# Attention and two gated MLPs on one core: a new instruction order from shaken latest-end times with named seeds

## The chip, the cores and the metric

The kernel runs on one core of one Trainium2 chip. The metric is the device time of one execution in microseconds, the median of three runs. An engine here is TensorE (PE, with its weight loads PEld), VectorE (DVE), ScalarE (ACT), GpSimd (POOL) or SyncE (SP, which issues the DMAs).

## The reference

Twelve heads of capped softmax attention for two batches of 448 tokens feed an RMS-normalised gated MLP and a second MLP, all in float32.

```python
scores = cap * np.tanh((scale * np.matmul(q, k.transpose(0, 1, 3, 2))) / cap)
attn = np.exp(scores - np.max(scores, axis=-1, keepdims=True))
attn = attn / (np.sum(attn, axis=-1, keepdims=True) + 1e-09)
x = tokens(np.matmul(attn, v))                      # 896 x 768
xn = x / np.sqrt(np.mean(x * x, axis=-1, keepdims=True) + 1e-06) * rms_g
g = xn @ w_gate                                     # 768 x 1536
h = (g * (1 / (1 + np.exp(-g))) * (xn @ w_val)) @ w_out
h2 = h @ w_in                                       # 768 x 2048
out = (h2 * (1 / (1 + np.exp(-h2)))) @ w_out2       # 2048 x 768
```

## The kernel before, in words

**Attention.** Twelve pairs of heads are worked on one after the other, overlapped. For a pair, PE computes scores in three chunks of 128 query rows for both heads (`qk`, L469: two products on half of the array's rows each) and one mixed chunk (L466); ACT takes the tanh (L476) and the exponential (L494); DVE caps and negates (`mx`, L484); PE transposes the probabilities (L559, L563, L561), DVE or ACT copies the transposes out (`ev`, L315), and PE multiplies them by the values (`pv`, L582: products on half of the array's columns, and L578). The row sums pass a small DVE operation (`guard`, L512) and a reciprocal; POOL spreads the reciprocals (L518, L523), and PE turns them (L529, L530). POOL also squares the results (L599, L600, L603), copies the mixed chunk's diagonal blocks (`diag`, L538) and computes the low parts of the first weights (L398).

**MLPs.** Products are made with float32r halves: each operand is split into a high part (a cast, L315) and a low part (a subtraction, L398, L675, L685), and one product is a triple of three matmuls (`passes`, L703; in the last matrix L1111). Seven products on sums of blocks take the place of eight (`group`); the sums of token blocks are called T1 to T4. Weights are loaded 768 columns at a time (`wraw`), unpacked by two ACT operations (L377, L380) and one DVE operation (L383), summed and split.

**What sets the order.** The kernel's operations are not emitted in the order of the code. The code records them in a `Plan` with costs for each engine that may run them, what they read and write, and which buffer they take. `place` lays them on the engines one by one: among those that can start within a small window it takes the one with the earliest due time (`prio`). `order` repeats this nine times, with due times that `dues` works back from the last placing, and keeps the placing whose last operation starts first. In the attention's plan 300 further tries add a random amount to 5% of the due times and keep what is no worse; the MLPs' plan (`rest`) has none. The instructions are then emitted in the order of the kept placing, and each engine runs its own in that order. A plan's costs set only the order and the choice of the engine; the chip keeps its own time. The first products of each MLP use `plain`, the others of this kind `group`; the gated MLP's output matrix, whose products go by `o` and a number, has its `mul` further down.

Of the kernel before, what the change touches and what calls it, by code (L numbers as in the profile page):

```python
# [2 lines left out]

# [25 lines left out]
CG = 12.0  # L29
WARM = 8  # L30
ROUNDS = 8
TRIES = 300
SHAKE = 2.0
SHARE = 0.05
XS = 0.5
PE = 6
TYH = 6.0
# [7 lines left out]
class Plan:  # L45
# [68 lines left out]
            due = min([end] + [ops[n]["prio"] for n in after[i]]) - cost  # L114
            o["prio"] = min(due, s) if e == "PE" else due

    def order(self, rounds=0, tries=0):

        users = self._link()
        best = None  # L120
        for n in range(rounds + 1):
            due = [o["prio"] for o in self.ops]
            out = self.place(users)
            if best is None or out[-1][0] < best[0][-1][0]:
                best = out, self.placed, due
            self.dues(users, self.placed)
        chance = random.Random(0)
        for n in range(tries):
            for o, due in zip(self.ops, best[2]):
                o["prio"] = due + (chance.gauss(0.0, SHAKE) if chance.random() < SHARE else 0.0)  # L130
            due = [o["prio"] for o in self.ops]
            try:
                out = self.place(users)
            except RuntimeError:
                continue
            if out[-1][0] <= best[0][-1][0]:
                best = out, self.placed, due
        self.placed = best[1]
        return best[0]

    def place(self, users):
# [84 lines left out]
def fused_kernel(ctx: ExitStack, tc: tile.TileContext, qkv, cap, g, wg, wv, wo, wi2, wo2, out):  # L226
# [61 lines left out]
    plan = Plan(TP, DUE, WIN, BIAS1)  # L288
# [458 lines left out]
        (sums if i else operands)(plan, u, v, 2 * i + 2)  # L747

    engines = {"PE": nc.tensor, "ACT": nc.scalar, "DVE": nc.vector, "Pool": nc.gpsimd, "SP": nc.sync, "none": None}
    order = plan.order(ROUNDS, TRIES)  # L750
    ends = max(n for n, (_, _, _, i) in enumerate(order) if plan.ops[i]["kind"] == "xe")
    for n, (_, _, e, i) in enumerate(order):
        plan.ops[i]["fn"](engines[e])
# [21 lines left out]
    def group(n, u, v, turn, x, outs, stag, pause=0):  # L775

        X, Y, Z, st = f"X_{n}", f"Y_{n}", f"Z_{n}", f"s_{n}"
        HK = KD // 2
        steps = (
            (X, f"w_{u}", 0, "11", True), (Z, f"w_{u}", DH, "21", True), (X, f"s_{u}", 0, "T2", False),  # L780
            (Y, f"w_{v}", 0, "T1", True), (X, f"s_{u}", DH, "T3", False), (X, f"w_{v}", DH, "T4", False),
            (Y, f"q_{u}", 0, "22", False),
        )
        c11, c12, c21, c22 = outs

        def product(n):
            ps, w, c, y, start = steps[n]
            for k in range(HK):
                def mul(e, k=k, n=n):
                    if start and k == 0:  # L790
                        bank(ps, ps[0])
                    passes(tl[ps][:, :S], w, c + k * P, (half(x(y, k), 0), half(x(y, k), 1)), start and k == 0, k == HK - 1, not start)

                op("mul", turn + 0.14 * n + 0.04 * k + (pause if n > 1 else 0), mul, {"PE": 0.595}, (f"h{w}", f"l{w}", x(y, k) + ".0", x(y, k) + ".1"), (ps,),
                   (take(ps, ps[0]),) if start and k == 0 else ())

        def keep(n, ps, i):
            def fn(e):
                if n == 0:
                    slot(st, stag)  # L800
                copy(e, f32(half(st, i)), tl[ps][:, :S])
            op("keep", turn + 0.1 * n, fn, {"ACT": 0.43, "DVE": 0.54}, (ps,), (f"{st}.{i}",), ((stag, 1, st),) if n == 0 else ())

        def add(ps, i, out):
            name, o, alloc = out
            op("add", turn, lambda e: nc.vector.tensor_add(o(), f32(half(st, i)), tl[ps][:, :S]), {"DVE": 0.54}, (ps, f"{st}.{i}"), (name,), alloc)

        product(0)
        keep(0, X, 0)
        product(1)  # L810
# [12 lines left out]
    def plain(n, u, v, turn, x, order, pauses=(0, 0, 0, 0)):  # L823

        HK = KD // 2
        left = {}
        at = 0
        for s, (c, tag, ys) in enumerate(order):
            ps = f"{tag}_{n}{c}"
            left[c] = left.get(c, 2)  # L830
            for y in ys:
                begin = left[c] == 2
                left[c] -= 1
                w, cols = f"w_{(u, v)[int(c[0]) - 1]}", DH * (int(y[0]) - 1)
                for k in range(HK):
                    def mul(e, k=k, y=y, ps=ps, w=w, cols=cols, begin=begin):
                        if begin and k == 0:
                            bank(ps, ps[0])
                        passes(tl[ps][:, :S], w, cols + k * P, (half(x(y, k), 0), half(x(y, k), 1)), begin and k == 0, k == HK - 1, not begin)

                    op("mul", turn + 0.14 * at + 0.04 * k + pauses[s], mul, {"PE": 0.595}, (f"h{w}", f"l{w}", x(y, k) + ".0", x(y, k) + ".1"), (ps,),
                       (take(ps, ps[0]),) if begin and k == 0 else ())
                at += 1
        return {c: f"{tag}_{n}{c}" for c, tag, _ in order}
# [93 lines left out]
    def both(n):  # L938
        return n + ".0", n + ".1"
# [42 lines left out]
    for i, n in enumerate(seq):  # L982
        tn = t0 + 0.857 * i
        pa, pb = PLACES[n]
        for x in {1: ("11",), 5: ("21", "22"), 2: ("12",)}.get(n, ()):
            for j in range(MH):
                convert(rest, ua(x, j), tn + 0.1 * j, to=atags[x].split()[j])
        for side, o, x, sign, y in SUMS.get(n, ()):
            if side == "a":
                for j in range(MH):  # L990
                    weight_sums(tn + 0.1 * j, f"wz_{ua(o, j)}", f"wz_{ua(x, j)}", sign, f"wz_{ua(y, j)}")
            else:
                for k in range(KH):
                    (ho, no), (hx, nx), (hy, ny) = (hb(z, k) for z in (o, x, y))
                    op("hsum", tn + 0.143 * k, lambda e, a=(ho, no), b=(hx, nx), c=(hy, ny): e.tensor_sub(*(f32(half(*z)) for z in (a, b, c))),
                       {"DVE": 0.54, "Pool": 1.1}, [f"{h}.{z}" for h, z in {(hx, nx), (hy, ny)} - {(ho, no)}], (f"{ho}.{no}",))
        for j in range(MH):
            weight_split(tn + 0.1 * j, ua(pa, j), f"o{n}_{j}", ("wh", "wl") if j < 2 else ("sh", "sl"))
        for k in range(KH):
            h, c = hb(pb, k)  # L1000
            halves(rest, ("hsh", "hsl"), tn + 0.143 * k, f"B{n}_{k}", btags[i % 2][k], (f"{h}.{c}", lambda h=h, c=c: f32(half(h, c))))
        bank_of = "XXZYXYXX"[n] if n != 2 else "Z"
        fresh = n in (1, 5, 2)
        for r in range(KH * MH):
            k, j = divmod(r, MH) if n != 4 else divmod(r, KH)[::-1]
            ps, w, x = f"{bank_of}_o{j}", f"o{n}_{j}", f"B{n}_{k}"

            def mul(e, k=k, ps=ps, w=w, x=x, fresh=fresh):
                if fresh and k == 0:
                    bank(ps, ps[0])  # L1010
                passes(tl[ps][:, :S], w, k * P, (half(x, 0), half(x, 1)), fresh and k == 0, k == KH - 1, not fresh)

            op("mul", tn + 0.0476 * r, mul, {"PE": 0.595}, (f"h{w}", f"l{w}", *both(x)), (ps,), (take(ps, ps[0]),) if fresh and k == 0 else ())
        for j in range(MH):
            X, Y, Z, tj = f"X_o{j}", f"Y_o{j}", f"Z_o{j}", tn + 0.7
            y0, y1 = f"y0_{j}", f"y1_{j}"
            if n == 1:
                evac("keep", tj, X, yf(0, j, 0), y0 + ".0", (ytags[0][j], y0))
            elif n == 6:
                evac("keep", tj, X, yf(0, j, 1), y0 + ".1")  # L1020
            elif n == 7:
                evac("keep", tj, X, yf(1, j, 0), y1 + ".0", (ytags[1][j], y1))
                evac("add", tj, Y, yf(1, j, 0), y1 + ".0", acc=True)
            elif n == 2:
                evac("add", tj, Z, yf(0, j, 0), y0 + ".0", acc=True)
            elif n == 3:
                evac("add", tj, Y, yf(0, j, 1), y0 + ".1", acc=True)
            else:
                evac("y", tj, X, yf(1, j, 1), y1 + ".1") if n == 4 else None
# [73 lines left out]
    def tokens_mul(turn, ps, a, w, k, start, stop, reads, more=False):  # L1103
# [6 lines left out]
            for r, (y, x) in enumerate(((ah, wh), (ah, wl), (al, wh))):  # L1110
                nc.tensor.matmul(out=tl[ps][:, :DH], lhsT=y, rhs=x, start=start and r == 0, stop=stop and r == 2, skip_group_check=more)  # L1111

        op("mul", turn, mul, {"PE": 0.52}, (f"h{w}", f"l{w}", *reads), (ps,), (take(ps, ps[0]),) if start else ())

    def rest_mul(turn, n, m, w, k, start, stop):
        g, _, _, c, i = rest_tile(m)
# [96 lines left out]
            evac("o", tn, f"Z_r{int(n == 3)}", o, name, (ktags[3], r) if n == 2 else (stile[0], r), w=DH)  # L1213
            store(tn, 2 * TH2, int(n == 3), o, name)

    for _, _, e, i in rest.order(ROUNDS):
        rest.ops[i]["fn"](engines[e])


# [59 lines left out]
```

## Time and profile before

| | |
|---|---|
| median of 3 runs | 596.53 us (596.52 to 596.63) |
| span of the profiled execution | 595.1 us |
| median less that span | 1.4 us |
| PE busy | 585.7 us (98%) |
| DVE busy | 512.1 us (86%) |
| ACT busy | 451.1 us (76%) |
| POOL busy | 58.7 us (10%), in the attention alone |

The span runs from the first to the last instruction of the one profiled execution; what lies around it belongs to the measured time as well. Busy times of PE are modelled at their ends, so a stretch can be counted busy and still hold a short wait; the distance from one matmul's start to the next tells more. The attention ends and the MLPs begin at about 143 us.

### The profile page before, as it was taken

To read this page: it belongs to the slowest core of one execution; us is meant where nothing else is said; L and a number is where in the kernel's file an instruction comes from. 1 tells how busy PE (TensorE), PEld (TensorE's weight loads), DVE (VectorE), ACT (ScalarE), POOL (GpSimd) and SP (SyncE) were. 2 spreads that over 40 slices of the span, in tenths; PEclk is the share of its full clock that TensorE was granted. 3 is DMA by queue.
4 is the path that set the end of the run, shared out by engine and by line. 5 is a ranking of instruction groups with operands and counts; after the bars stand their busy time and mean duration, and the time that the engine had idled before them with its cause. 6 is when DMAs were issued, how large, how long until landed. Compare 5 with 4: busy or idle time off the path is not lost.

```text
span 595.1 us, 8525 instructions
## 1 busy us (share of the span) xinstructions
PE 585.7 (98%) x3056; PEld 495.5 (83%) x3056; DVE 512.1 (86%) x934; ACT 451.1 (76%) x800; POOL 58.7 (10%) x92
## 2 busy tenths in 40 slices
PE   8999999999999999999999999999999999999997
PEld 4555565557889999999999998998999999999997
DVE  4799997994999989888699999999877898999991
ACT  5999878983858777776698685777888899986641
POOL 1234561552000000000000000000000000000000
PEclk9999999999999999999999999999999999999999
DMA  7123311310024435443445200423534455440101
GB/s 265 54 106 107 107 56 53 139 75 0 2 106 160 160 108 168 150 143 123 160 167 187 72 0 2 159 61 114 197 113 159 156 209 178 155 145 1 41 26 68
DMA packets 15626, 66.22 MB, mean 111 GB/s; under 512 B 1888, under 2 KB 3680, under 8 KB 15584
## 3 DMA queue, kind: packets, MB, share of 16 engines
q1 hardware_dynamic: 15552, 65.67, 31.3%
q8 instruction: 24, 0.39, 0.3%
q14 instruction: 18, 0.15, 0.1%
q0 software_dynamic: 32, 0.00, 0.0%
HBM read 62.92 MB, written 2.75 MB: 110 GB/s over the span
## 4 chain that ended last, share of the span: by engine, by line
PE 88%; DVE 7%; ACT 3%; issue 1%; DMA 1%; SPq 0%; DVEq 0%; ACTq 0%
PE X L703 28%; PE Y L703 16%; PE Z L703 9%; PE X L1111 8%; PE av L582 5%; PE pt L559 5%; PE Y L1111 5%; PE s L469 5%; PE Z L1111 2%; PE s L466 2%; PE av L578 1%; PE pt L563 1%; PE pt L529 1%; DVE wl L398 1%; DMA x<-in_qkv 1%
## 5 line engine op out<-in xcount | busy, mean ns | idle before, releaser
L380 ACT ACTIVATE wraw<-wraw 128x768 uint32<-128x768 uint16 x68 | 61.8, 908 | 0.0
L703 PE MATMUL X<-q,sh 128*128 128x448 f32 x198 | 56.5, 365 | 0.6 <-DVE q L685 0.6
L484 DVE TENSOR_SCALAR_CACHE_REDUCE p<-p,ncap 128x448 f32<-128x448 f32 x72 | 45.9, 673 | 6.5 <-ACT p L476 6.3
L398 DVE TENSOR_TENSOR wl<-wz,wh 128x768 fp32r<-128x768 f32 x47 | 44.8, 954 | 6.4 <-ACT wh L315 6.3
L703 PE MATMUL X<-p,wh 128*128 128x448 f32 x174 | 49.8, 367 | 0.0
L315 ACT CAST wh<-wz 128x768 fp32r<-128x768 f32 x46 | 38.3, 834 | 12.0 <-DVE wz L418 4.5
L703 PE MATMUL X<-q,wh 128*128 128x448 f32 x162 | 46.2, 366 | 0.6 <-ACT p L315 0.6
L383 DVE SCALAR_TENSOR_TENSOR wz<-wz,wraw 128x768 uint32<-128x768 uint32 x44 | 42.0, 955 | 4.0 <-ACT wraw L380 3.8
L315 DVE COPY pe<-pt 128x448 f32<-128x448 f32 x72 | 41.3, 619 | 4.1 <-PE pt L563 3.7
L315 ACT COPY p<-X 128x448 f32<-128x448 f32 x45 | 24.0, 532 | 26.9 <-PE X L703 25.9
L703 PE MATMUL Z<-p,wh 128*128 128x448 f32 x150 | 42.9, 367 | 0.0
L377 ACT ACTIVATE wz<-wraw 128x768 f32<-128x768 f32 x44 | 40.1, 911 | 3.8 <-DMA wraw<-in_wi 1.6
L315 ACT CAST q<-p 128x448 fp32r<-128x448 f32 (+1 forms) x54 | 29.0, 547 | 17.8 <-PE X L1111 5.9
L476 ACT ACTIVATE p<-s,tscl 128x896 f32<-128x896 f32 x36 | 34.9, 1004 | 9.7 <-PE s L469 9.6
L703 PEld LDWEIGHTS X<-q,sh 128*128 128x128 f32 x198 | 37.2, 188 | 4.2 <-DVE q L685 1.0
L315 ACT CAST p<-p 128x448 fp32r<-128x448 f32 (+1 forms) x50 | 27.1, 552 | 12.6 <-DVE p L693 4.7
L703 PE MATMUL X<-q,sl 128*128 128x448 f32 x99 | 36.2, 366 | 0.0
L703 PEld LDWEIGHTS X<-p,wh 128*128 128x128 f32 x174 | 32.5, 188 | 2.8
L469 PE MATMUL s<-x 64*128 64x448 f32 x144 | 34.0, 574 | 0.3 <-ACT p L476 0.3
L703 PEld LDWEIGHTS X<-q,wh 128*128 128x128 f32 x162 | 30.3, 188 | 3.6 <-ACT p L315 1.0
L703 PE MATMUL X<-p,wl 128*128 128x448 f32 x87 | 31.8, 366 | 0.0
L582 PE MATMUL av<-pe,x 128*64 128x448 f32 x144 | 31.4, 552 | 0.0
(257 smaller groups left out, 1654.3 us busy)
## 6 DMA issues: line engine op xcount, KB each, us to landing
wraw<-in_wo SPq DMA_DIRECT2D x28, 768.0 KB, 4.3
wraw<-in_wi SPq DMA_DIRECT2D x16, 768.0 KB, 4.3
wraw<-in_wg SPq DMA_DIRECT2D x12, 768.0 KB, 5.8
wraw<-in_wv SPq DMA_DIRECT2D x12, 768.0 KB, 4.3
x<-in_qkv SPq DMA_DIRECT2D x11, 512.0 KB, 3.9
x<-in_qkv SPq DMA_DIRECT2D x14, 256.0 KB, 4.2
out<-q SPq DMA_DIRECT2D x12, 192.0 KB, 1.8
out<-zq SPq DMA_DIRECT2D x2, 192.0 KB, 1.9
```

The source lines that it names most:

```text
L315: e.tensor_copy(out=o, in_=i) if e is nc.vector else e.copy(out=o, in_=i)
L377: e.activation(out=z, in_=high.bitcast(F32), func=ACTF.Prelu, scale=2.0 ** -112, alpha=2.0 ** 32)
L380: e.activation(out=t["low"], in_=t["half"], func=ACTF.Copy, scale=2.0 ** -13, bias=2.0 ** -14 - 0.5)
L383: e.scalar_tensor_tensor(t["zu"], t["zu"], 3, t["low"], ALU.logical_shift_left, ALU.bitwise_or)
L398: e.tensor_sub(new(l, pool(), [P, w], F32R, tags[1], bufs=bufs), z(), tl[h])
L469: nc.tensor.matmul(out=ps[:, s, :S], lhsT=q_of(p, s, c), rhs=k_of(p, s), start=True, stop=True)
L476: nc.scalar.activation(out=o, in_=i, func=ACTF.Tanh, scale=tscl)
L484: nc.vector.tensor_scalar(t, t, ncap, None, ALU.mult, ALU.min, accum_out=tl[nb][:, n:n + 1])
L559: nc.tensor.transpose(ps[:, c * P:(c + 1) * P], pc[:, a:a + P], ident)
L582: nc.tensor.matmul(out=tl[av][s * D:(s + 1) * D, :S], lhsT=v[:, (2 * k + s) * D:(2 * k + s + 1) * D], rhs=tl[f"pe_{p}_{m}"], start=k == 0, ...
L703: nc.tensor.matmul(out=ps, lhsT=a, rhs=y, start=start and r == 0, stop=stop and r == 2, skip_group_check=more)
L1111: nc.tensor.matmul(out=tl[ps][:, :DH], lhsT=y, rhs=x, start=start and r == 0, stop=stop and r == 2, skip_group_check=more)
```

## The change

No operation is added or removed: both programs have 2836 matmuls. `order` takes a list of named seeds. Each seed gives, by a small generator of its own, one share of the due times that are moved (1% to 10%) and one width (1 to 4), and adds to these due times a sum of three uniform numbers; the start is always the best placing so far, and a placing is kept when its end is no later. The end is now that of the last operation to end, not the last to start. The attention's plan gets 58 seeds in place of the 300 tries, and the MLPs' plan, which had none, gets 34. In the MLPs' plan a triple is charged 0.613 instead of 0.595, and one of the last matrix 0.523 instead of 0.52.

```diff
-TRIES = 300
-SHAKE = 2.0
-SHARE = 0.05
+SHAKES = 2.0, 4.0, 1.0
+SHARES = 0.05, 0.02, 0.1, 0.01
+SEEDS1 = (
...
+    def shaken(self, due, seed):
+
+        mask, share, shake = (1 << 64) - 1, SHARES[seed % 4], SHAKES[seed // 4 % 3]
...
+        return [d + shake * (2 * (chance() + chance() + chance()) - 3) if chance() < share else d for d in due]
+
+    def order(self, rounds=0, seeds=()):
...
+        for seed in seeds:
+            due = self.shaken(best[1], seed)
+            for o, d in zip(self.ops, due):
+                o["prio"] = d
+            out = self.place(users)
+            if end(out) <= end(best[0]):
+                best = out, due
...
-    order = plan.order(ROUNDS, TRIES)
+    order = plan.order(ROUNDS, SEEDS1)
...
-                op("mul", turn + 0.14 * n + 0.04 * k + (pause if n > 1 else 0), mul, {"PE": 0.595}, (f"h{w}", f"l{w}", x(y, k) + ".0", x(y, k) + ".1"), (ps,),
+                op("mul", turn + 0.14 * n + 0.04 * k + (pause if n > 1 else 0), mul, {"PE": 0.613}, (f"h{w}", f"l{w}", x(y, k) + ".0", x(y, k) + ".1"), (ps,),
...
-    for _, _, e, i in rest.order(ROUNDS):
+    for _, _, e, i in rest.order(ROUNDS, SEEDS2):
```

Everything moves a little; four things can be read from the new order. The lines of the changed kernel are 25 higher (L469 is L494 there, L582 is L607, L703 is L728).

**Blocks of tiled products.** On PE, row-tiled score products and column-tiled value products stand in blocks between transposes and full products. Up to the first MLP product, the order before has 24 blocks of score products and 19 of value products; the changed order has 22 and 15. PE in the second pair of heads, before:

```order
L582 MATMUL av<-pe,x_132 64x448 x4
L559 MATMUL pt<-ident,p_246 128x128
L529 MATMUL pt<-ident,rr 128x128 x3
L530 MATMUL pt<-fold,mr 128x64
L559 MATMUL pt<-ident,p_279 128x128
L559 MATMUL pt<-ident,p_287 128x128
L561 MATMUL pt<-fold,pmm_96 128x64
L559 MATMUL pt<-ident,pc_373 128x128
L466 MATMUL s<-x_310 128x448
L582 MATMUL av<-pe,x_132 64x448 x2
```

PE at the same place in the changed kernel:

```order
L588 MATMUL pt<-ident,pm 128x128
L607 MATMUL av<-pe,x_132 64x448 x6
L584 MATMUL pt<-ident,p_241 128x128
L491 MATMUL s<-x_318 128x448
L584 MATMUL pt<-ident,pc_336 128x128
```

The six value products of this pair stand in one block where they stood in two.

**The end of the attention.** DVE works on the last pair's capped scores; `thm` is the mixed chunk, `p8`, `p12` and `p20` the full ones, and `av` the value product of the pair before. DVE before:

```order
L315 COPY pe_1533<-pt_1506 128x448
L484 TENSOR_SCALAR p8_1460,nb_1509<-p8_1460,ncap_90 128x448
L484 TENSOR_SCALAR p20_1504,nb_1509<-p20_1504,ncap_90 128x448
L484 TENSOR_SCALAR p12_1467,nb_1509<-p12_1467,ncap_90 128x448
L484 TENSOR_SCALAR thm_1444,nb_1509<-thm_1444,ncap_90 128x448
L484 TENSOR_SCALAR p20_1504,nb_1509<-p20_1504,ncap_90 128x448
L594 TENSOR_TENSOR p19_1569<-av_1528,p7_1558 128x448
```

DVE in the changed kernel:

```order
L340 COPY pe_1539<-pt_1515 128x448
L509 TENSOR_SCALAR thm_1419,nb_1488<-thm_1419,ncap_90 128x448
L509 TENSOR_SCALAR p8_1473,nb_1488<-p8_1473,ncap_90 128x448
L509 TENSOR_SCALAR p12_1481,nb_1488<-p12_1481,ncap_90 128x448
L509 TENSOR_SCALAR p20_1517,nb_1488<-p20_1517,ncap_90 128x448
L619 TENSOR_TENSOR p19_1564<-av_1536,p7_1534 128x448
```

The mixed chunk moved from last but one of the scores to the first of these four, and its exponential on ACT from last but one to fourth from the end.

**The first group of MLP products.** `q0`, `q1` and `q2` hold the three tiles of the token sum T2, `q3` to `q5` those of T1; `p0` is a token tile. PE before:

```order
L703 MATMUL X_1731<-q0_1736,sh_933 128x448 x2
L703 MATMUL X_1731<-q0_1736,sl_1015 128x448
L703 MATMUL X_1731<-q1_1760,sh_933 128x448 x2
L703 MATMUL X_1731<-q1_1760,sl_1015 128x448
L703 MATMUL Y_1789<-q3_1722,wh_930 128x448 x2
L703 MATMUL Y_1789<-q3_1722,wl_940 128x448
L703 MATMUL X_1731<-q2_1779,sh_933 128x448 x2
```

PE in the changed kernel; `q9` is a normalised token tile of the second batch:

```order
L728 MATMUL X_1713<-q0_1755,sh_1230 128x448 x2
L728 MATMUL X_1713<-q0_1755,sl_1295 128x448
L728 MATMUL Z_1778<-q9_1705,wh_549 128x448 x2
L728 MATMUL Z_1778<-q9_1705,wl_623 128x448
L728 MATMUL X_1713<-q1_1767,sh_1230 128x448 x2
L728 MATMUL X_1713<-q1_1767,sl_1295 128x448
L728 MATMUL Y_1790<-q3_1731,wh_1091 128x448 x2
```

Another product's triple stands between T2's first and second. On ACT, some ten microseconds later in this group, before (the copy of `X_1731` frees a sum for PE's next products; the casts ahead of it are high parts of T4 and wait for DVE's subtractions):

```order
L315 CAST q9_1857<-p15_581 128x448
L853 ACTIVATE p13_1866<-X_1807 128x448
L315 CAST q10_1873<-p16_824 128x448
L315 CAST q11_1883<-p16_824 128x448
L315 COPY p8_1754<-X_1731 128x448
```

ACT in the changed kernel:

```order
L340 CAST q9_1856<-p15_573 128x448
L878 ACTIVATE p13_1865<-X_1803 128x448
L340 CAST wh_1874<-wz_1684 128x768
L340 COPY p8_1761<-X_1713 128x448
L340 CAST q10_1887<-p16_808 128x448
```

The copy now stands ahead of the casts of `q10` and `q11`.

**POOL and ACT around them.** Before, POOL ran the low part of a weight unit right behind the diagonal copies of the fifth pair; in the changed order no low part stands behind such a copy. On ACT, the load of the activation table for the MLPs stood ahead of the first cast of a normalised tile; now it stands behind two of them. Three copies or casts move from DVE to ACT and one subtraction from DVE to POOL, all in the attention's plan.

## Rows read from the trace of the kernel before

**Rows 1.** The page: busy time, share and instructions of each engine.
```profile
PE 585.7 (98%) x3056; PEld 495.5 (83%) x3056; DVE 512.1 (86%) x934; ACT 451.1 (76%) x800; POOL 58.7 (10%) x92
```

**Rows 2.** The chain that ended last: start, length, engine, tile, line, records.
```profile
17.79 1.70 PE s L469 x8
...
33.11 0.90 PE av L582 x4
34.27 0.95 PE s L469 x4
...
98.91 2.41 PE av L582 x12
...
221.41 4.28 PE X L703 x21
```

**Rows 3.** Timeline of PE at 104 us: start, length, what, idle before.
```profile
103.95 0.27 PE L563 MATMUL pt<-swap,pm 128*128 128x128 f32 x1
104.06 0.27 PE L563 MATMUL pt<-ident,pm 128*128 128x128 f32 x1
104.26 1.77 PE L469 MATMUL s<-x 64*128 64x448 f32 x8
```

**Rows 4.** Timeline of 58 to 62 us, four rows.
```profile
58.06 1.81 POOL L398 TENSOR_TENSOR wl<-wz,wh 128x768 fp32r<-128x768 f32 x1
58.08 1.82 DVE L512 TENSOR_SCALAR sm<-sm 128x7 f32<-128x7 f32 x1 [0.68 <-ACT pc L494]
...
61.14 2.21 DVE L315 COPY pe<-pt 128x448 f32<-128x448 f32 x4
...
61.81 0.55 PE L559 MATMUL pt<-ident,pc 128*128 128x128 f32 x3 [0.62 <-DVE pe L315]
```

**Rows 5.** Timeline of PE at the end of the attention.
```profile
134.78 0.60 PE L559 MATMUL pt<-ident,p 128*128 128x128 f32 x4
...
135.68 0.44 PE L563 MATMUL pt<-ident,pm 128*128 128x128 f32 x2 [0.30 <-ACT pm L494]
...
136.33 0.33 PE L559 MATMUL pt<-ident,p 128*128 128x128 f32 x1 [0.21 <-ACT p L494]
...
137.31 1.14 PE L582 MATMUL av<-pe,x 128*64 128x448 f32 x4
138.38 0.87 PE L559 MATMUL pt<-ident,p 128*128 128x128 f32 x6
```

**Rows 6.** Waits of the weight loads in the MLPs: us in total, times, longest.
```profile
PEld X L703 <- ACT p L315: 1.0, 1, 1.0
PEld X L703 <- DVE q L685: 1.0, 1, 1.0
...
PEld Y L703 <- DVE p L954: 0.5, 1, 0.5
PEld X L703 <- ACT q L315: 0.4, 1, 0.4
...
PEld Z L1111 <- DVE wl L398: 0.4, 1, 0.4
```

**Rows 7.** Timeline of PE at 157 us: T2's second triple and the next.
```profile
156.97 0.37 PE L703 MATMUL X<-q,sh 128*128 128x448 f32 x1
...
157.96 0.48 PE L703 MATMUL X<-q,sh 128*128 128x448 f32 x1 [0.62 <-DVE q L685]
...
158.48 0.57 PE L703 MATMUL Y<-q,wh 128*128 128x448 f32 x2
```

**Rows 8.** Timeline of ACT at 148 us: the load of the activation table.
```profile
148.42 1.28 ACT L853 ACT_TABLE_LOAD   x1 [4.76 <-PE X L703]
...
149.71 0.55 ACT L853 ACTIVATE p<-X 128x448 f32<-128x448 f32 x1
```

**Rows 9.** Windows: length, busy us of PE, PEld, DVE, ACT, POOL, clock, DMA.
```profile
345.00:360.00 15.00, 14.84 (x73) 13.32 (x72) 14.94 (x24) 13.01 (x23) 0.00 (x0) 1.00 0.00 0
...
540.00:555.00 15.00, 15.00 (x87) 15.00 (x86) 14.95 (x24) 11.10 (x20) 0.00 (x0) 1.00 0.00 0
```

More of the change, by code (lines that the diff above doesn't have):

```diff
@@ L1 @@
-import random
 from contextlib import ExitStack
@@ L31 @@
 ROUNDS = 8
-TRIES = 300
-SHAKE = 2.0
-SHARE = 0.05
+SHAKES = 2.0, 4.0, 1.0
+SHARES = 0.05, 0.02, 0.1, 0.01
+SEEDS1 = (
[4 rows of a table added]
+)
+SEEDS2 = (
+    2000003, 2000011, 2000012, 2000017, 2000019, 2000026, 2000037, 2000041, 2000051, 2000054, 2000059, 2000061, 2000081, 2000086, 2000100, 2000113,
+    2000116, 2000129, 2000133, 2000137, 2000147, 2000183, 2000237, 2000243, 2000257, 2000324, 2000336, 2000355, 2002639, 2002669, 2002681, 2002751,
+    2002761, 2003937,
+)
 XS = 0.5
@@ L115, in dues, with chance, end @@
             o["prio"] = min(due, s) if e == "PE" else due
-    def order(self, rounds=0, tries=0):
+    def shaken(self, due, seed):
+        mask, share, shake = (1 << 64) - 1, SHARES[seed % 4], SHAKES[seed // 4 % 3]
+        x = (seed * 0x9E3779B97F4A7C15 + 0x1234567) & mask
+        x ^= x >> 29
+        def chance():
+            nonlocal x
+            x ^= x << 13 & mask
+            x ^= x >> 7
+            x ^= x << 17 & mask
+            return (x >> 11) / 2.0 ** 53
+        for _ in range(4):
+            chance()
+        return [d + shake * (2 * (chance() + chance() + chance()) - 3) if chance() < share else d for d in due]
+    def order(self, rounds=0, seeds=()):
         users = self._link()
         best = None
+        def end(out):
+            return max(s + self.ops[i]["on"][e] for s, _, e, i in out)
         for n in range(rounds + 1):
@@ L123, in order @@
             out = self.place(users)
-            if best is None or out[-1][0] < best[0][-1][0]:
-                best = out, self.placed, due
+            if best is None or end(out) < end(best[0]):
+                best = out, due
             self.dues(users, self.placed)
[L127 to L138, printed above, removed]
+        for seed in seeds:
[4 more added lines that the diff above has]
+            if end(out) <= end(best[0]):
+                best = out, due
         return best[0]
@@ L839, in mul @@
                         passes(tl[ps][:, :S], w, cols + k * P, (half(x(y, k), 0), half(x(y, k), 1)), begin and k == 0, k == HK - 1, not begin)
-                    op("mul", turn + 0.14 * at + 0.04 * k + pauses[s], mul, {"PE": 0.595}, (f"h{w}", f"l{w}", x(y, k) + ".0", x(y, k) + ".1"), (ps,),
+                    op("mul", turn + 0.14 * at + 0.04 * k + pauses[s], mul, {"PE": 0.613}, (f"h{w}", f"l{w}", x(y, k) + ".0", x(y, k) + ".1"), (ps,),
                        (take(ps, ps[0]),) if begin and k == 0 else ())
@@ L1011, in mul @@
                 passes(tl[ps][:, :S], w, k * P, (half(x, 0), half(x, 1)), fresh and k == 0, k == KH - 1, not fresh)
-            op("mul", tn + 0.0476 * r, mul, {"PE": 0.595}, (f"h{w}", f"l{w}", *both(x)), (ps,), (take(ps, ps[0]),) if fresh and k == 0 else ())
+            op("mul", tn + 0.0476 * r, mul, {"PE": 0.613}, (f"h{w}", f"l{w}", *both(x)), (ps,), (take(ps, ps[0]),) if fresh and k == 0 else ())
         for j in range(MH):
@@ L1111, in mul @@
                 nc.tensor.matmul(out=tl[ps][:, :DH], lhsT=y, rhs=x, start=start and r == 0, stop=stop and r == 2, skip_group_check=more)
-        op("mul", turn, mul, {"PE": 0.52}, (f"h{w}", f"l{w}", *reads), (ps,), (take(ps, ps[0]),) if start else ())
+        op("mul", turn, mul, {"PE": 0.523}, (f"h{w}", f"l{w}", *reads), (ps,), (take(ps, ps[0]),) if start else ())
     def rest_mul(turn, n, m, w, k, start, stop):
```

4 rows, old and new, of the table SEEDS1 are left out of this document.

## The prediction

> **What bounds the kernel now.** I read the busy times first. PE is busy for 585.7 of 595.1 us [rows 1], so whatever the order does, it can only take out time in which PE stands still or works at less than its pace. So I looked next for PE's pace: in the chain that ended last, a run of 21 float32r matmuls, seven triples, takes 4.28 us, 0.611 us a triple [rows 2]. In most of the MLPs PE keeps that pace without a break, and there a new order is worth nothing. The triple was charged 0.595 in the old plan; the new charge, 0.613, is nearer to the row. That changes no duration: it gives the plan the right idea of how fast the other engines must be.
>
> Then I listed the places where PE does not keep its pace. In the MLPs the view of waits has five long ones of the weight loads, three for DVE and two for ACT [rows 6]. In the attention the losses are of three kinds: a restart at each block of tiled products [rows 2, 3], one delay at 62 us [rows 4], and waits at the end, where no next pair is left to fill them [rows 5]. The change does no work less, so its worth is the sum of what it takes from these places, less what it puts in new ones. Tail and start carry the same operations as before.
>
> **The change part by part.**
>
> *The five waits in the MLPs.* They are 1.0, 1.0, 0.5, 0.4 and 0.4 us, 3.3 in all [rows 6]. What one costs PE is seen at 157 us: a triple of X on T2 starts at 156.97, its second matmul only at 157.96, and the next triple at 158.48 [rows 7]. That is 1.51 us from triple to triple where 0.61 is the pace, so this wait of 1.0 cost 0.9. I take 0.1 less than the wait for each of the five: 3.3 - 0.5 = 2.8 us. Does the new order remove them? At 157 us the second tile of T2 was late from DVE. The new order puts a triple that needs no sum, on `q9`, between the first and second of T2: 0.6 us of cover. The product that broadcasts the norm's reciprocal, on which DVE's chain waits, stands behind three triples instead of four after the last sum of squares: another 0.6. Together 1.2 against 0.9 lost. At 171 us PE waited for a copy on ACT, the first of the five [rows 6]; it stood behind two casts that waited for DVE's differences; now it stands ahead of them and behind a cast of weights. The other three are short waits (0.4 to 0.5) for a DVE or ACT operation that comes one or two places too late, and the MLPs' plan had no shaken tries to move such places at all. I take 2.8. The bounds: 0, if each wait comes back at another place, and 3.1, if the small restarts after each wait go as well.
>
> *Blocks in the attention.* Four records of a score block take 0.95 us, eight take 1.70 [rows 2]: four more cost 0.75, so each block carries 0.20 beside its work. For value products four take 0.90 and twelve 2.41 [rows 2]: 0.755 for each further four, so 0.15 a block. Entering a block costs as well: two transposes start 0.11 apart, and the first score product 0.20 after the last of them, 0.09 more [rows 3]. The new order has two score blocks and four value blocks fewer: 2 x 0.29 + 4 x 0.24 = 1.5 us. Below, this could be 0.6 where a block now ends at a place at which PE waits anyway; above, 1.5.
>
> *The delay at 62 us.* DVE's guard of the row sums, an operation on 7 columns, started at 58.08 and took 1.82 us, beside a POOL subtraction of 1.81 that had started 0.02 before it [rows 4]. So the guard was held until POOL's operation had ended, and everything behind it on DVE with it: the reciprocal, a score operation, the scaling and the copies of transposes, of which the first began at 61.14. PE waited 0.62 us for one of these copies [rows 4]. In the new order POOL's low parts of weights stand behind no diagonal copy, so none of them starts just ahead of a guard in this way. I take 0.7 with the restart. It can come back where POOL's other subtractions and squares stand near a guard, so the bounds are -0.7 (one more such meeting than before) and 0.7.
>
> *The end of the attention.* With four transposes at 0.11, PE was through at 135.22 and went on at 135.68, when ACT gave the mixed chunk's exponential: 0.46. Two transposes further, at 135.90, it waited until 136.33: 0.43. A block of four value products, 0.95 at the most from 137.31, was left at 138.38: some 0.2 [rows 5]. The new order brings the mixed chunk forward on DVE and on ACT, so that the exponentials that come last are those of the full chunks, whose transposes PE can do one by one. I take these 1.1 us. The bounds are 0, since ACT still has six exponentials to do after the last tanh, and 1.4, should the short waits between go too.
>
> *What moves beside it.* Three copies go from DVE to ACT and one subtraction from DVE to POOL. ACT has 24% of the span free and POOL 90% [rows 1], and ACT's share lies beside PE's products of the same pair. I set this at nothing; without that cover three copies at some 0.5 us would be 1.5 us late, which lies in the range. The weight loads keep their number and size.
>
> *The activation table.* Its load on ACT takes 1.28 us; ACT had then stood idle for 4.76, and the first silu of the MLPs starts 0.01 after it [rows 8]. So it cost nothing before. In the new order it stands behind two casts of normalised tiles, and the casts of T1 and T2 come behind it. PE's first T2 triple stands 18 triples behind the first product, some 11 us, so I take it as covered, at 0, with 1.3 us, the whole load, as the other bound. The Trainium skill ("ScalarE: Activation LUTs", section "What ACT_TABLE_LOAD costs") counts a drain of about 1.38 us on top of the 1.28, 2.66 in all. The trace has the 1.28 and no drain behind it [rows 8]. By the page the uncovered load would be 1.4 us dearer than by the row.
>
> **The sum.** 2.8 + 1.5 + 0.7 + 1.1 = 6.1 us. The profiled execution has a span of 595.1, 1.4 less than the median of the runs, and nothing outside the span changes. So 589.0 us of span and 596.5 - 6.1 = 590.4 us measured.
>
> **The rivals.**
>
> *The MLPs' waits come back elsewhere.* In the stages with seven products on sums DVE has little slack: from 540 to 555 us it is busy for 14.95 of 15 [rows 9]. An order that brings one subtraction forward there pushes another back by 0.6 to 0.9 us. For it: three of the five waits are for DVE. Against it: in that same window PE has no wait at all, so a full DVE is not yet a late one. Then only the attention gains: 3.3 us, 593.2; with half of the waits gone 591.8.
>
> *The attention gains only its blocks.* Who waits for whom there depends on meetings of a few hundredths of a microsecond, as at 58.08, which no list of due times can hold to. For it: 0.02 us decided 0.7. Against it: the end of the attention is no meeting but a place in two queues. Then 2.8 + 1.5 = 4.3 us, 592.2.
>
> *The table load shows.* Its place in the queue is as above; its worst price is 1.3 us, so 591.7. By the page of the Trainium skill named above it would be 2.7 us and 593.1. Against both: what stands between it and PE's first need of a cast behind it.
>
> *Slower: DVE runs dry in the last matrix and in the output matrix.* Where DVE is full, every microsecond for which the new order lets it wait, for a weight load or for a cast on ACT, is a microsecond at the end. From 345 us on it is busy for over 14.9 of 15 in five windows, of which [rows 9] has the first and the last. If DVE stood idle for 1.5 us more in each, the loss would be 7.5 us, and with the gain of 6.1 the kernel would come out at 597.9. It decides from 1.2 us a window. Against it: the same engine with the same operations is in order now with 0.05 idle in such a window, and the new charge makes the plan leave it no less room than it really has.
>
> *The order is new but the time is not.* The waits are 3.3 us in the MLPs and some 2 in the attention; should as many arise anew, only the blocks' 1.5 us and at worst nothing would be left: 595 to 596.5.
>
> **How the numbers follow.** Forecast, with the gain between 5.0 and 7.6 us (588.9 to 591.5): 0.66. MLPs' waits back in whole or half, 591.8 to 593.2: 0.14. Attention with blocks alone, 592.2: 0.08. Table load, 591.7: 0.05. No change: 0.04. Slower: 0.03. The predicted time is 590.4. A range from 588.4 to 592.8 leaves out the two last, the fuller form of the first rival, and gains beyond 8.1 us, which would need all upper bounds at once (3.1 + 1.5 + 0.7 + 1.4 = 6.7) and waits at the start as well that I have not priced. A measurement of this kernel tells some 0.2%, 1.2 us, from no change: faster by more than that 0.93, within it 0.04, slower 0.03.
>
> **What would show it.** In the new profile the five waits of [rows 6] should be gone and none over 0.5 us come in their place; from the first MLP product to the last matmul 2.8 us less should pass. The attention should end some 3.3 us earlier, near 140 us, with the chain's score and value blocks longer, no guard over 1 us, and no gap over 0.2 us before PE in its last 8 us. The load of the table should have a cast ahead of it, not 4.76 us of idling. I am wrong if waits of PE for DVE appear in the windows where DVE is full, if a guard meets a POOL operation of 2 us, or if the attention still ends at 143 us.

## The result and the profile after

The changed kernel takes 590.58 us, the median of 4 runs (589.77 to 591.86), beside 596.58 for the kernel before (4 runs, 596.52 to 596.64). The ratio is 0.9896, with a 95% interval of 0.9879 to 0.9913. Forecast were 590.4.

The profiled execution has a span of 587.7 us, where that of before has 595.1. Its page first: busy times, and the shares in the chain that ended last.

```profile
PE 580.4 (99%) x3056; PEld 496.6 (85%) x3056; DVE 508.2 (86%) x930; ACT 453.4 (77%) x803; POOL 61.0 (10%) x93
...
PE 97%; ACT 1%; DMA 1%; DVE 0%; SPq 0%; issue 0%; DVEq 0%
```

The chain's shares in the kernel before:

```profile
PE 88%; DVE 7%; ACT 3%; issue 1%; DMA 1%; SPq 0%; DVEq 0%; ACTq 0%
```

Beside [rows 1], PE's share of the span goes from 98 to 99% with the same 3056 records. The work is the same; the breaks in it are fewer. DVE and ACT hold 1% of the chain between them, where they held 10%: PE hardly follows from another engine's end any more.

Where the time went is read best by stretches, each from one PE start to another. A pair's last full value product (L578 before, L603 after) marks the end of its work on PE. The mark between attention and MLPs is the first product of the norm's sums of squares (L631 before, L656 after), at 142.92 and 138.79 us; the expectations below call it the first MLP product, and the first MLP triple follows 0.7 us behind it.

| stretch | before, us | after, us | difference |
|---|---|---|---|
| first score product starts | 5.42 | 5.56 | +0.14 |
| to the first full-score block (mixed product x2) | 1.53 | 1.27 | -0.26 |
| to the first pair's full value product | 17.85 | 17.55 | -0.30 |
| to the norm's first product (attention, other eleven pairs) | 118.12 | 114.41 | -3.71 |
| to the end of the last matmul (rest of the norm, MLPs) | 448.67 | 445.33 | -3.34 |

So the attention gave 3.71 + 0.30 = 4.0 us and the MLPs 3.34. The sum, 7.35, is the difference of the spans, 7.4 (the first two rows nearly cancel); the medians differ by 6.0, of which more below.

The waits of the weight loads after, of the steps of the norm (L669, L656) and of the MLPs (L728; the last matrix, L1136, has none):

```profile
PEld pt L669 <- POOL ri L664: 0.5, 1, 0.5
PEld Y L656 <- issue: 0.4, 2, 0.2
...
PEld Y L728 <- DVE p L831: 0.3, 1, 0.3
```

All five waits of [rows 6] are gone, and one of 0.3 us has come. The wait of 0.5 lies at 84 us, in the attention, and PE itself has no gap there. The two windows in which DVE was full before have it as full now, but PE still has no gap. The columns are those of [rows 9].

```profile
345.00:360.00 15.00, 15.00 (x75) 13.84 (x74) 14.91 (x25) 11.60 (x21) 0.00 (x0) 1.00 0.01 2
540.00:555.00 15.00, 15.00 (x87) 15.00 (x86) 14.76 (x25) 9.52 (x18) 0.00 (x0) 1.00 0.01 1
```

The place of [rows 7], on PE's timeline after: T2's first triple, one of `q9`, T2's second, and the next.

```profile
152.23 0.57 PE L728 MATMUL X<-q,sh 128*128 128x448 f32 x2
152.64 0.36 PE L728 MATMUL X<-q,sl 128*128 128x448 f32 x1
152.84 0.57 PE L728 MATMUL Z<-q,wh 128*128 128x448 f32 x2
153.25 0.36 PE L728 MATMUL Z<-q,wl 128*128 128x448 f32 x1
153.45 0.57 PE L728 MATMUL X<-q,sh 128*128 128x448 f32 x2
...
154.06 0.57 PE L728 MATMUL Y<-q,wh 128*128 128x448 f32 x2
```

They start 0.61 apart, the pace of [rows 2]. The table's load on ACT's timeline, which answers to [rows 8]:

```profile
145.88 1.11 ACT L340 CAST q<-p 128x448 fp32r<-128x448 f32 x2 [4.78 <-issue]
147.01 1.28 ACT L878 ACT_TABLE_LOAD   x1
148.30 0.55 ACT L878 ACTIVATE p<-X 128x448 f32<-128x448 f32 x1
```

It stands behind two casts now and ends some 4 us before T2's first triple, so it still hides.

In the attention, the blocks first: rows of the chain that ended last (start, length, engine, tile, line, records).

```profile
29.01 2.41 PE av L607 x12
...
119.18 1.65 PE av L607 x8
...
128.14 2.41 PE av L607 x12
135.09 2.41 PE av L607 x12
```

Nine pairs have their twelve records of value products in one block and three have them in two. Now the end, on PE's timeline, beside [rows 5]:

```profile
132.54 0.27 PE L588 MATMUL pt<-ident,pm 128*128 128x128 f32 x1
132.84 0.52 PE L584 MATMUL pt<-ident,p 128*128 128x128 f32 x3
133.19 0.27 PE L588 MATMUL pt<-swap,pm 128*128 128x128 f32 x1
...
135.02 2.48 PE L607 MATMUL av<-pe,x 128*64 128x448 f32 x12
137.43 0.55 PE L554 MATMUL pt<-ident,rr 128*128 128x128 f32 x3
```

One transpose takes 0.11 at pace, so the gap ahead of 132.84 is 0.19, and it is the only one above 0.06 between transposes. Last the guard of the row sums, all twelve of them by their line (ns shortest/median/longest, first and last start), before and after:

```profile
L512 DVE TENSOR_SCALAR sm<-sm x12: 160/172/1822, 16.7 to 138.4; 128x7 f32<-128x7 f32 x12
```

```profile
L537 DVE TENSOR_SCALAR sm<-sm x12: 157/160/882, 16.2 to 134.8; 128x7 f32<-128x7 f32 x12
```

The longest one after on the timeline, with what meets it and who waits in the end:

```profile
80.35 0.99 POOL L443 TENSOR_TENSOR wz<-wz 128x384 f32<-128x384 f32 x1
80.49 0.88 DVE L537 TENSOR_SCALAR sm<-sm 128x7 f32<-128x7 f32 x1
...
82.82 0.55 PE L584 MATMUL pt<-ident,pc 128*128 128x128 f32 x3 [0.26 <-DVE pe L340]
```

The guard of 1.82 us in [rows 4] is gone. Another one, of the seventh pair, meets POOL's sum of two halves of a weight unit: it starts 0.14 after the sum and ends 0.03 after it, and PE waits for a copy behind it at 82.82.

### The profile page after: what moved, and what is told of

Same layout as the page of the kernel before. It is cut to its first block, busy times and chain, and to the rows that moved or that the text cites. A ratio compares the mean times of both kernels' runs of the same rounds, so it can differ in the third digit from the quotient of the medians.

```text
span 587.7 us, 8518 instructions
## 1 busy us (share of the span) xinstructions
PE 580.4 (99%) x3056; PEld 496.6 (85%) x3056; DVE 508.2 (86%) x930; ACT 453.4 (77%) x803; POOL 61.0 (10%) x93
## 4 chain that ended last, share of the span: by engine, by line
PE 97%; ACT 1%; DMA 1%; DVE 0%; SPq 0%; issue 0%; DVEq 0%
PE X L728 31%; PE Y L728 16%; PE Z L728 10%; PE X L1136 9%; PE Y L1136 6%; PE s L494 5%; PE pt L584 5%; PE av L607 5%; PE Z L1136 3%; PE s L491 2%; PE av L603 2%; PE pt L588 1%; PE pt L554 1%; DMA x<-in_qkv 1%; PE pt L586 0%; PE pt L555 0%
## 5 line engine op out<-in xcount | busy, mean ns | idle before, releaser
L728 PE MATMUL X<-q,sh 128*128 128x448 f32 x198 | 56.4, 366 | 0.0
L728 PE MATMUL X<-p,wh 128*128 128x448 f32 x174 | 49.7, 367 | 0.0
L423 DVE TENSOR_TENSOR wl<-wz,wh 128x768 fp32r<-128x768 f32 x46 | 43.5, 952 | 6.3 <-ACT wh L340 6.2
L728 PE MATMUL X<-q,wh 128*128 128x448 f32 x162 | 46.0, 365 | 0.0
L340 ACT CAST wh<-wz 128x768 fp32r<-128x768 f32 x48 | 40.0, 833 | 7.7 <-DVE wz L443 5.4
L728 PE MATMUL Z<-p,wh 128*128 128x448 f32 x150 | 42.8, 366 | 0.0
L728 PEld LDWEIGHTS X<-q,sh 128*128 128x128 f32 x198 | 37.2, 188 | 3.3
L728 PE MATMUL X<-q,sl 128*128 128x448 f32 x99 | 36.1, 365 | 0.0
L728 PEld LDWEIGHTS X<-p,wh 128*128 128x128 f32 x174 | 32.5, 188 | 2.7
L494 PE MATMUL s<-x 64*128 64x448 f32 x144 | 33.5, 571 | 0.3 <-ACT p L501 0.3
L728 PEld LDWEIGHTS X<-q,wh 128*128 128x128 f32 x162 | 30.4, 188 | 2.6
L728 PE MATMUL X<-p,wl 128*128 128x448 f32 x87 | 31.9, 366 | 0.0
L1136 PE MATMUL X<-wh,q 128*128 128x384 f32 x108 | 31.1, 338 | 0.0
```

Source lines behind the costliest of these rows:

```text
L340: e.tensor_copy(out=o, in_=i) if e is nc.vector else e.copy(out=o, in_=i)
L423: e.tensor_sub(new(l, pool(), [P, w], F32R, tags[1], bufs=bufs), z(), tl[h])
L494: nc.tensor.matmul(out=ps[:, s, :S], lhsT=q_of(p, s, c), rhs=k_of(p, s), start=True, stop=True)
L728: nc.tensor.matmul(out=ps, lhsT=a, rhs=y, start=start and r == 0, stop=stop and r == 2, skip_group_check=more)
```

## The experiments

The predicted steps were tested one by one; where a ratio is given, it is against the kernel before on the same chip (median 597.22 of 17 runs in the first group, 596.89 of 9 in the last). The four versions between these groups (the delay undone, the cut blocks, T2's cover, ACT's copy) were executed once each and are read by their stretches.

**The changed kernel again.** No edit.

> The changed kernel itself, once more. Its four times lay at two levels, 589.8 and 591.3 to 591.9, while the kernel before stays within 0.12 us. Theory: the upper level is a delay of 1.5 to 2 us that some executions have and others have not, so the times again fall near 589.8 and near 591.5, with little between. Rival: the times are spread evenly, as from many small waits of varying length; then they fill the stretch between 589.5 and 592.

589.31 us, ratio 0.9863 [0.9844, 0.9883]; attention after the first pair 114.43, MLPs 445.39. The two stretches repeat to 0.1 us, while the single times do not: runs of this kernel lie between 589.2 and 591.9, and on this chip the kernel before spread as well, from 596.3 to 599.1. So the theory of two levels that belong to the changed kernel fell; what makes the spread is sought at the start, below.

**The attention's new order alone.** In the MLPs' plan, old charges and no seeds:

```diff
-    for _, _, e, i in rest.order(ROUNDS, SEEDS2):
+    for _, _, e, i in rest.tried(ROUNDS):
-{"PE": 0.613} ... {"PE": 0.523}
+{"PE": 0.595} ... {"PE": 0.52}
```

> The new order in the attention alone; the MLPs keep the order and the charges of before. Theory (the two parts add up): 3.3 us by the forecast and 4.1 by the two profiles, so 592.4 to 593.2, and the MLPs' five waits of 3.3 us are all back. Rival (the gain sits in the MLPs, where all waits have gone): under 2 us, over 594.5. If the two levels of the changed kernel come from the attention's order, they show here as well, some 1.7 apart.

592.66 us, ratio 0.9921 [0.9902, 0.9941]. Attention 114.43 as in the full change, MLPs 448.71 as before.

**The MLPs' new order alone.** The attention's plan with the old 300 tries:

```diff
-    order = plan.order(ROUNDS, SEEDS1)
+    order = plan.tried(ROUNDS, TRIES)
```

> The new order and charges in the MLPs alone; the attention keeps the order of before. Theory: 2.8 by the forecast and 3.3 by the two profiles, so 593.3 to 593.8. Rival (the table load or a full DVE gives some of it back): over 594.5. If the two levels of the changed kernel come from the MLPs, where nothing is left to take up a late weight or a late cast, they show here; if they come from the attention, the times agree within 0.3.

593.22 us, ratio 0.9932 [0.9911, 0.9952]. Attention 118.14, MLPs 445.37. The two parts touch nothing of each other, and their gains, 0.79% and 0.68%, sum to 1.47%, beside 1.37% for the whole on this chip: the same within the intervals.

**The charges alone.** The kernel before with 0.613 and 0.523 in the MLPs' plan, and no seeds.

> The kernel before with the new charges alone (0.613 and 0.523), no shaken tries in the MLPs. Theory: the two waits at the MLPs' start (2.0 us) need the shaken order and stay; some of the three short ones (1.3 us) go with the right charge, so 595.3 to 596.5. Rival: the charge is what counts, and all five go: 593.3 to 593.8.

596.38 us, ratio 0.9989 [0.9975, 1.0003]; MLPs 448.36, 0.3 less than before. Its waits in the MLPs:

```profile
PEld X L703 <- ACT p L315: 1.6, 2, 1.1
PEld X L703 <- DVE q L685: 1.0, 1, 1.0
PEld Y L703 <- DVE p L954: 0.7, 1, 0.7
```

Both waits of 1.0 at the MLPs' start stay. Some 0.3 of the 3.3 us at most come with the charge alone; the rest needs the seeds (the seeds without the charge were not tried).

**The delay at 62 us, undone in the kernel before.** One low part of a weight unit is put behind the spreads of the reciprocals (`mr`) of the fifth pair, so that it no longer starts just ahead of the guard:

```diff
+    order = behind(order, <low part lw_1>, <mr_4>)
```

> The kernel before, with one POOL operation moved: the weight's low part that met the fifth pair's guard now stands behind that pair's two spreading operations. Theory (the meeting held DVE, and PE lost 0.7 by it): the guard takes some 0.17 us instead of 1.82, and the stretch from the first pair's full value product to the first MLP product, 118.1 us in the kernel before, takes 117.4. Rival (PE had something else to wait for there, or the operation now meets another one): 118.1 or more.

595.8 us, beside 596.68 for the kernel before. The guard fell as expected, and the time from the fifth pair's full value product to the next fell from 10.24 to 9.55: 0.69.

```profile
57.67 0.17 DVE L521 TENSOR_SCALAR sm<-sm 128x7 f32<-128x7 f32 x1 [0.68 <-ACT pc L503]
...
59.04 1.83 POOL L407 TENSOR_TENSOR wl<-wz,wh 128x768 fp32r<-128x768 f32 x1
```

The same guard takes 0.17 once the subtraction of 1.83 starts behind it.

**Six blocks cut in two.** In the changed kernel, for six pairs, a transpose is put behind the first value product of a block of three, so that twelve records become four and eight:

```diff
+    order = behind(order, <a transpose>, <first value product of the block>)   # six pairs
```

> The changed kernel, with one transpose moved into each of six blocks of three value products, so that each block falls into one and two. Theory (a block costs 0.24 beside its work): the stretch from the first pair's full value product to the first MLP product grows by 1.4 us, from 114.4 to 115.8. Rival (a block's overhead lies beside waits that PE has anyway): under 0.4 more. If the moved transposes are missed by DVE or ACT, more than 2.

Attention after the first pair 116.95, where the changed kernel has 114.41: 2.54 more. From full value product to full value product, the six pairs take 0.86, 0.35, 0.34, 0.34, 0.34 and 0.30 more. In five of them the block alone shows, so a value block costs about 0.33, not 0.24. In the first the weight loads of the block's second part wait besides, 0.59 and 0.34 us, for DVE's copy of the transpose that was moved. That, and the larger cost of a block, is why 2.54 stand where 1.4 were expected.

**T2's cover taken away.** In the changed kernel T2's second triple goes ahead of that of `q9`:

```diff
+    last = behind(last, <T2's second triple>, <T2's first triple>)
```

> The changed kernel, with T2's second triple put back ahead of the triple on q9 that stands before it, as in the order before. Theory (0.6 of the 1.2 us of cover is this triple, the wait was 0.9): a wait for DVE of 0.2 to 0.4 returns at T2's second triple, and the MLPs take 0.3 us more than the 445.3 of the changed kernel. Rival (the earlier broadcast alone covers it): no wait and the same time. Rival (the triple alone covers it): 0.9.

MLPs 445.83, 0.5 more than in the changed kernel, and of the waits:

```profile
PEld X L737 <- DVE q L719: 0.6, 1, 0.6
```

The wait of [rows 6] is back with 0.6 of its 1.0, and the loss is 0.5 where 0.3 was expected. The order of the triples was worth 0.5 of the 0.9 us lost there. The other 0.4 is T2's second tile being ready earlier: DVE ends its low part 1.55 us after the start of T2's first triple in the kernel before (157.91 and 156.36), 1.10 here (153.01 and 151.91). The earlier broadcast of the reciprocal is the likely reason (not tried by itself).

**ACT's copy put back.** In the changed kernel the copy of `X` stands behind one cast of T4 again. The addition that reads the copy stays where it was and now comes ahead of it, so one block of the value branch gets other values.

```diff
+    last = behind(last, <copy of X>, <cast of T4's first high part>)
```

> The changed kernel, with ACT's copy of the first sum of X in the second group put back behind one cast of T4, the one that it now stands ahead of. Theory (the copy's place in ACT's queue is what cost 0.9 at 171 us): a wait of the weight loads for ACT of some 0.5 to 1.0 returns there, and the MLPs take that much more, less 0.1. Rival (the new order has room there): no wait and no change.

MLPs 446.36, 1.0 more, with the wait back:

```profile
PEld X L737 <- ACT p L349: 1.3, 1, 1.3
```

The copy starts at 167.60, as the cast ends; the addition, which it now has to follow too, had ended at 167.49. So the cast held it.

**The new meeting taken away.** In the changed kernel POOL's sum is put behind the spreads of the seventh pair:

```diff
+    order = behind(order, <sum of wz_3.0>, <mr_6>)
```

> The changed kernel, with the POOL sum that met the seventh pair's guard (0.88 us, PE waited at 82.8) put behind that pair's two spreading operations. Theory (as with the fifth pair in the kernel before): the guard takes some 0.17 us, PE loses 0.4 less, and the stretch from the first pair's full value product to the first MLP product takes 114.0 instead of 114.4. Rival (the sum is then late for the weights' later parts or meets another operation): 114.4 or more.

588.75 us (588.65 to 588.91), ratio 0.9861 [0.9845, 0.9877]. Attention after the first pair 114.00, 0.41 less. The twelve guards:

```profile
L546 DVE TENSOR_SCALAR sm<-sm x12: 157/160/198, 15.6 to 133.8; 128x7 f32<-128x7 f32 x12
```

None is held for more than 0.04 us. The forecast, 0.4, is the difference of the stretch. The median is the lowest of all versions, but it comes from another chip than the 589.31 of the changed kernel, and the ratios to the kernel before, 0.9861 and 0.9863, do not tell the two apart: the stretch shows the gain, not the median.

**The start.** Before the attention PE runs warm-up products; with more of them, PE should not be idle before the first scores. Three kernels: the changed one with 10 instead of 8, the one of the sum with 10, and the one of the sum with 13.

```diff
-WARM = 8
+WARM = 10
```

> The changed kernel with ten warming products at the start instead of eight, so that PE is busy until the first input has landed. In the profiles so far the first score product took 0.92 to 1.77 us and the first pair ended between 24.1 and 26.5. Theory (PE's slow pace after the idle time between the warming products and the first score product is what spreads the times): the first score products take 0.9 and 0.86 in every profile, the first pair ends near 24.3, and the times lie within 0.5 us of each other, near 589.5. Rival (the spread comes from the loads): the first product begins 0.4 later and the times spread over 1.5 to 2.5 as before.

590.21 us (589.49 to 590.62), ratio 0.9884 [0.9867, 0.99].

> The two edits together: the sum moved and ten warming products. Theory: the gains add, 0.4 us under the kernel with ten warming products alone, near 589.1. Rival: the meeting only moves, and the time is that of the other.

589.84 us, ratio 0.9879 [0.9862, 0.9896].

> The sum moved and thirteen warming products. They last until some 7.3 us, so that the first score product starts 1.7 us later than it could. Theory: PE is at full pace when the scores come, so they take 0.9 and 0.86, but the first pair ends near 25.6, and the times are 1.2 us above those with ten, with as little spread. Rival: PE's pace at that point does not hang on what it did before, and the first product's length varies as it did.

589.48 us, ratio 0.9873 [0.9857, 0.989].

None beats the version of the sum with 8. With 10 the first score product came at 5.91 and 5.79, with 13 at 5.83, where 8 gave 5.34 to 5.80. PE's idle time before it is gone, yet in one of them its first record still ran at half the pace, and the times of that version spread by 1.1 us, not 0.5; this theory fell. The two forecasts for the version of the sum were missed as well: 589.84 with 10, where 589.1 was expected, and with 13 less than that, not 1.2 more. The 7.3 us for the start with 13 had no room for the further warm-up products being faster: they start 0.21 us apart until 4.5 us and 0.11 apart from there on. The execution of the sum with 10 that was profiled has 446.08 for its MLPs, 0.7 to 0.8 more than the others with the new order, and its trace says why. ACT, then DVE, then PE around 310 us, from three views of the timeline by engine:

```profile
307.57 0.91 ACT L411 ACTIVATE q<-wraw 128x768 f32<-128x768 f32 x1 [2.16 <-DMA wraw<-in_wo]
...
309.30 0.96 DVE L417 SCALAR_TENSOR_TENSOR q<-q,wraw 128x768 uint32<-128x768 uint32 x1 [0.95 <-ACT wraw L414]
...
316.71 0.67 PE L737 MATMUL Z<-q,wh 128*128 128x448 f32 x2 [0.46 <-DVE p L989]
```

In the version of the sum alone ACT waits 1.22 us for this weight unit, and DVE not at all:

```profile
306.07 0.91 ACT L411 ACTIVATE q<-wraw 128x768 f32<-128x768 f32 x1 [1.22 <-DMA wraw<-in_wo]
```

Here ACT starts on the unit 1.5 us later. All that stands before it in the same order is 0.5 later, so the unit itself came some 1.0 late; DVE stood idle for 0.95, and PE waited 0.8 (the weight loads' view) seven microseconds further on.

## Why the prediction was right

**MLPs, 2.8 predicted, 3.34 measured,** which is over the upper bound of 3.1. All five waits are gone and one of 0.3 has come. From start to start of PE's records the five cost 0.90, 0.90, 0.43, 0.32 and 0.36, 2.9 in all, and the new one costs 0.24. So the waits gave 2.7, as the term had it. The other 0.7 is in no wait. It is spread over the 2279 steps from one record to the next: 572 of them take 0.207 to 0.216 us before and 461 after, and no run tells why. That the new order and not the charge removes the two waits at the start is shown by the charge alone, which keeps both; that their places matter is shown by the two edits that bring them back. The cover at T2 was less than worked out: with the triple of `q9` taken away 0.5 us are lost again, so the earlier tile gave 0.4 of the 0.9 where I had counted 0.6 for the earlier broadcast.

**Blocks, 1.5 predicted.** The mechanism was right, and the size was off by more than that of any other term. A value block costs 0.30 to 0.35 by the cut blocks, where the term had 0.24. What it left out stands behind a block, as in the changed kernel at 37 us:

```profile
37.34 1.77 PE L494 MATMUL s<-x 64*128 64x448 f32 x8
39.05 0.33 PE L584 MATMUL pt<-ident,pc 128*128 128x128 f32 x1
39.21 0.49 PE L554 MATMUL pt<-ident,rr 128*128 128x128 f32 x3
39.54 0.33 PE L555 MATMUL pt<-fold,mr 128*128 128x64 f32 x2
```

The record behind the block's first transpose starts 0.16 after it, the three behind that 0.11 apart: another 0.05. With it a value block comes to 0.30 and a score block to 0.35. The number was off too. In the stretch of the eleven pairs value blocks fall from 18 to 13 (the first pair took one more) and score blocks from 21 to 19: 5 x 0.3 + 2 x 0.35 = 2.2. Adding up all steps from record to record in this stretch gives 2.6 that is in no wait; most of the rest is places where a full product stands right behind a block (six before, three after, 0.1 each). Score blocks were not cut by themselves.

**The delay at 62 us, 0.7 predicted, 0.69 measured** in the kernel before with that meeting alone undone. But a new meeting, of the lower bound's kind and smaller, took 0.4 back, as the version without it shows. The text named what would bring it: POOL's other operations near a guard.

**The end, 1.1 predicted.** Of the three losses in [rows 5], 0.46, 0.43 and 0.2, one gap of 0.19 is left: 0.9. This is read from the rows; no run isolates it.

With these sizes the attention's terms give 2.6 + 0.7 - 0.4 + 0.9 = 3.8, and the stretch gained 3.71. Its waits (steps over 0.04 above the usual one between the same kinds of record) sum to 2.0 us before and 0.9 after, all of them in the places named here. The first pair gained 0.30 besides, which no term had.

**What was to cost nothing cost nothing.** The table load hides behind the casts. The Trainium skill ("ScalarE: Activation LUTs", section "What ACT_TABLE_LOAD costs") counts a drain of about 1.38 us besides the 1.28 of the load. The trace does not agree here: the load starts 0.02 after the cast ahead of it ends and takes 1.28, and the first activation starts 0.01 behind it. Its rival was out for another reason, the 4 us of cover.

**The rivals.** No wait came back over 0.3 in the MLPs, and the attention gained 1.1 us in waits besides its blocks. The slower one, that DVE runs dry, showed itself only in the execution in which a weight unit was 1.0 us late: 0.95 of idle DVE cost PE 0.8. So its mechanism and its price (nearly one to one) are right, and the order of the change by itself does not set it off.

**Why the median was so near.** The terms sum to 6.1 and the trace holds 7.35. The medians of the first comparison differ by 6.0, but those on the other chip by 7.9 (597.22 to 589.31). One step of the sum did not hold: that nothing outside the span changes. Wherever span and time of one execution are both on record, 1.7 to 1.9 us lie outside the span in the kernel before, and also with one of the two new orders, but 2.1 to 2.2 with both. No run tells where these 0.3 us go. The 1.4 that I took set the span of one execution beside the median of others; with 1.8 the execution that was profiled comes to 596.9, 0.3 above the median. The changed kernel's profiled execution is the fastest of its four, 0.8 below their median. So 7.4 - 0.3 - 0.3 - 0.8 = 6.0. The forecast's distance of 0.2 us from the median is thus partly luck: the gain was under-counted by 1.2 us, and these runs hid as much.

## What to carry to other kernels

When the bounding engine is busy for 98%, list each place where it leaves its pace, price each from start to start, and add them: here that gave 6.1 of 7.35 us. The largest terms were two waits of a microsecond, which a change of one or two places in a queue removes, and the blocks, whose price must count what stands before and behind them. Look for small operations of one engine that grow from 0.16 to 0.9 or 1.8 us beside an operation of another; a search of orders that does not know of such meetings removes one and makes the next, and a single moved operation (0.4 us here) can then beat the search. Set a single median beside stretches of the trace between fixed marks: behind the start they repeated to 0.1 us here, with one exception that had its own cause, where the runs spread by 2.

## What the runs showed of the hardware

**The first products' pace varies from run to run.** The same two records of the mixed product take from 0.92 to 1.83 us. There are two paces, one half of the other: a record of this product starts 0.88 or 0.46 us after the one ahead of it, a warm-up product 0.21 or 0.11. What varies is when the slow pace ends: at 4.5 us in the execution with 13 warm-up products, by 5.4 in the version of the sum, at 10.7 in that of the attention's order alone. From PE's timeline of the attention's order alone:

```profile
5.80 1.83 PE L519 MATMUL s<-x 128*128 128x448 f32 x2 [0.65 <-DMA x<-in_qkv]
7.56 4.05 PE L522 MATMUL s<-x 64*128 64x448 f32 x12
```

and of the version of the sum:

```profile
5.36 0.99 PE L500 MATMUL s<-x 128*128 128x448 f32 x2 [0.23 <-DMA x<-in_qkv]
6.28 1.82 PE L503 MATMUL s<-x 64*128 64x448 f32 x8
```

By the time of the first pair's full value product they are 2.66 us apart (26.49 and 23.83). The granted clock of the windows from 5 to 12 us reads 1.00 in both, so the rows do not tell why; keeping PE busy before did not settle it. The first of these executions took 594.93 us, the other five of its kernel 592.27 to 592.97, so the start is likely most of the spread among runs of one kernel; the others left no trace that could show it.

**This DVE operation on 7 columns is held for as long as a POOL operation that started before it runs:** 1.82 us beside one of 1.81 [rows 4], 0.88 beside one of 0.99. In the kernel before three more guards are held so, for 0.66, 0.69 and 0.33 us in all, two by squares and one by a subtraction. Each ends 0.02 to 0.03 us after POOL's operation, and PE waits behind none of these three. In the version of the sum, where no such operation runs on for 0.2 us, the guard takes 0.16 to 0.20 in twelve of twelve places. Other DVE operations do not show it: the capping (`mx`, L484 before) takes 0.67 us when POOL is busy at its start (24 times) and 0.68 when it is not (60).
